# Two early output rows held back, and remainders of fills moved to GpSimd, in a four-layer attention and Fourier kernel

## The chip, the cores and the metric

The kernel runs on one core of a Trainium2 chip. Its time is the device time of one execution in microseconds (us), as the median of several runs; a profiled execution is a further run with the hardware profiler on. TensorE multiplies matrices into eight banks of PSUM, VectorE, ScalarE and GpSimd work elementwise, and SyncE (SP in the profile) issues the DMAs. Each engine takes its instructions in the order in which the program has them.

## The reference

The input x has 2048 rows of 640 values. Four layers follow each other: attention, Fourier, attention, Fourier.

```python
def _A_ref(x, wqkv, wo):
    H = 32; Dh = D // H; W = 256
    q, k, v = ...                      # x @ wqkv, 32 heads of 20
    scores = einsum("bhqd,bhkd->bhqk", q, k) * (Dh ** -0.5)
    mask = (idx[:, None] - idx[None, :] >= 0) & (idx[:, None] - idx[None, :] < W)
    p = softmax(where(mask, scores, -1e9))
    o = einsum("bhqk,bhkd->bhqd", p, v)
    return o.transpose(...).reshape(B, S, D) @ wo

def _B_ref(x, dft_seq_re, dft_seq_im, dft_hid_re, dft_hid_im):
    a = einsum("bsd,ed->bse", x, dft_hid_re)
    b = einsum("bsd,ed->bse", x, dft_hid_im)
    return einsum("ts,bse->bte", dft_seq_re, a) - einsum("ts,bse->bte", dft_seq_im, b)

x = x + _A_ref(_layernorm(x), A_wqkv, A_wo)
x = x + _B_ref(_layernorm(x), ...)
x = x + _A_ref(_layernorm(x), A_wqkv, A_wo)
x = x + _B_ref(_layernorm(x), ...)
```

## The kernel before, in words

Every product of two float32 matrices is made of three products of parts: each operand is split into a rounded part (hi) and a remainder (lo = value - hi), and hi x hi, hi x lo and lo x hi are summed in one PSUM bank. ScalarE usually makes the hi part and another engine the remainder. Many instructions on VectorE, ScalarE and GpSimd are such pairs.

**An attention layer** has four stretches. `before_heads` computes V and the first Q and K columns. `heads` is a software-pipelined loop over 8 quads of heads times 16 blocks of 128 query rows, so 128 steps after ten lead steps (`LEAD`). In a step TensorE makes four score products for the row maxima (`s_head`, line 622), whose maxima VectorE takes (line 627); four transposed score products (`t_pair`, line 650), whose exponentials ScalarE takes (line 660) and whose band GpSimd masks (`t_mask`, lines 666 and 670); and the products of the previous step's probabilities with V (`pv`, line 685).

Between these, `fill` puts pieces of other work on TensorE, once a step. First come the remaining Q and K columns: ten chunks of 128 columns, of which chunks 2 to 9 are made here (`pieces`, `lockstep`, line 253, 64-row half products in pairs), with four results of 128 x 512 each, so 32 results a layer. ScalarE copies a result out (line 540), GpSimd rounds it into the tile `c` (line 543), VectorE makes the remainder (`sub_job`, line 207), and SP stores both to `qk_d` (line 520), from where `pack` loads them into `qp` and `kp` for a later quad (line 585).

Next come the early output rows (`partials`): 16 row blocks, each the product of the first three fifths of o with `wo` (`EARLY = 3`, 36 half products), added to the layer's input (line 970). Last come the late output rows (`late`): the other two fifths (12 products), added to that (line 1064 inside the loop, 1070 after it), then mean, variance and normalization. The operands of both are loaded from `o_d` by `load_o` in sets of four row blocks, scaled by the reciprocal row sums (line 885, two halves on GpSimd, or line 873), cut into hi and lo (lines 215 and 207).

`after_heads` makes what is left of the early rows, then the late rows, and between them the first products of the Fourier layer (`unit`, `seq`, line 1360), which need normalized rows. `gather` (lines 1412 to 1431) copies the Fourier accumulators out.

**How order is set.** The order is written out by hand through a clock of half steps: `tick` advances `self.slot`, runs what `post(delay, fn)` has put off, and takes one job from each of three queues (`lanes` act, dve, pool). `job` appends to a queue, or runs the function at once when the loop is over (`self.after`). After the loop, `spend` turns estimated TensorE time into ticks.

```python
for lane in self.lanes.values():
    if lane and lane[0][0] <= self.slot:
        lane.popleft()[2]()
```

The choice of fill in the loop is `more`: projections, then all early rows, then late rows while their operands are ready. The function `fourier_hook` takes over tiles for the Fourier layer as late rows finish.

Of the kernel before, what the change touches and what calls it, by code (L numbers as in the profile page):

```python
# [8 lines left out]
F32R = mybir.dt.float32r  # L9
BF16 = mybir.dt.bfloat16  # L10
AF = mybir.ActivationFunctionType
OP = mybir.AluOpType
# [22 lines left out]
RATE = 4  # L35
FIRST = 7
LATE = 9
PACE = 0.65

STEP = 2.5  # L40
# [23 lines left out]
class Net:  # L64
# [107 lines left out]
    def tick(self):  # L172
        self.slot += 1
        for k in sorted(k for k in self.posted if k <= self.slot):
            for f in self.posted.pop(k):
                f()
        for lane in self.lanes.values():
            if lane and lane[0][0] <= self.slot:
                lane.popleft()[2]()

    def job(self, lane, key, fn):

        if self.slot is None or self.after:
            fn()
        else:
            self.lanes[lane].append((self.slot + 1, key, fn))
# [11 lines left out]
    def sub_job(self, lane, key, lo, src, hi, done=None):  # L198

        eng = {"dve": self.nc.vector, "pool": self.nc.gpsimd}[lane]  # L200
        n = 2 if lane == "pool" else 1
        w = src.shape[-1] // n
        for i in range(n):
            c = slice(i * w, (i + 1) * w)

            def sub(c=c, last=i == n - 1):
                eng.tensor_tensor(out=lo[..., c], in0=src[..., c], in1=hi[..., c].bitcast(F32), op=OP.subtract)  # L207
                if last and done:
                    done()
            self.job(lane, key, sub)  # L210
# [141 lines left out]
    def attention(self, xsrc, xdst):  # L352
        self.take_small(F32)
        for name in ("kp", "qp"):
            for i in (1, 0):
                if (name, i) != ("kp", 0):
                    self.take_qk(name, i)
        self.after, self.wide, self.lead = False, False, True
        self.late_o, self.late_t, self.part_t, self.packable = [], 0, 0, set()
        self.before_heads(xsrc)  # L360
        self.heads(xsrc, xdst, self.fourier_hook)
        self.after_heads()
# [160 lines left out]
    def pieces(self, c, sbs, role):  # L523

        self.flush(("w", c))
        w = self.turn["w", c]
        sets, of = [], {}
        for sb in sbs:
            xt = self.xnt(sb)
            if sb % 2 == 0:  # L530
                sets.append(([], []))
            p = self.bank(role)
            of[id(p)] = p, sb, self.last_bank
            sets[-1][0].append(p)
            sets[-1][1].append([((w[:, 0, k, :], w[:, 1, k, :]), (xt[:, 0, k, :], xt[:, 1, k, :])) for k in range(KC)])

        def copied(p, sb):
            st = self.work.tile([P, 2, 512], F32R, name="c", tag="c", bufs=3)
            r = self.raw()[:, :512]
            self.nc.scalar.activation(r, p, AF.Copy)  # L540

            def cast():
                self.nc.gpsimd.tensor_copy(st[:, 0, :], r)  # L543
# [3 lines left out]
            def store():  # L547
                self.store_qk(c, sb, st)
                self.packable.add((c, sb))
            self.job("pool", ("qk", c, sb), cast)  # L550
# [46 lines left out]
    def heads(self, xsrc, xdst, hook):  # L597
# [123 lines left out]
        self.rest = self.late(xsrc, xdst, hook)  # L721
        self.stored = set()
        self.slot = 0
        made = [0]
        early = 6 * EARLY * NB

        def relieve():
            while self.heavy:
# [2 lines left out]
        def more():  # L731

            r = next(self.proj, None)
            if r is not None:
                done[0] += r
                return r
            if not self.left and not self.ready_part():
                return None
            r = next(self.out, None)
            if r is not None:  # L740
                made[0] += r
                return r
            return next(self.rest, None) if self.left or self.ready_late() else None

        def fill(n):

# [21 lines left out]
        steps = 16 * NQ  # L768
        self.ring6 = dict.fromkeys((0, 1, 2, 3), -99.0)
        for step in range(-LEAD, steps + 1):  # L770
            now[0] = step
            clock = step * STEP
            if step == -1:
                self.ring6.update({4: -99.0, 5: -99.0})
# [18 lines left out]
            if done[0] < total:  # L793
                nf = max([FIRST if t < -2 else RATE + (t < 0)]
                         + [(d - done[0]) / max(1, at - s) for at, d in due])
            elif made[0] < early:
                nf = LATE
# [37 lines left out]
    def load_o(self, o, sb, k, raw=None, rr=None):  # L835

        nc = self.nc
        h0, h1, d0, d1 = CHUNKS[k]
        o["left"] = o.get("left", 0) + 1
        if not self.after and not all((q, sb) in self.stored for q in range(h0 // 4, h1 // 4)):  # L840
            def again():
                o["left"] -= 1
                self.load_o(o, sb, k, raw, rr)
            self.post(1, again)
            return
        for q in range(h0 // 4, h1 // 4):
# [36 lines left out]
        def half(i):  # L883
            cs = slice(i * 256, (i + 1) * 256)
            nc.gpsimd.tensor_tensor(out=raw[:, cs], in0=raw[:, cs], in1=rr[:, cs], op=OP.mult)
            if i:
                parts()
        for i in range(2):
            self.post(7, lambda i=i: self.job("pool", key, lambda: half(i)))

    def let_go(self):

# [104 lines left out]
    def poll_late(self, n):  # L997
# [16 lines left out]
            self.cut_to(0)  # L1014
        sb = len(self.late_o)
        if (n > 6 and sb < NSB and (NQ - 1, sb) in self.stored and (self.after or sb < 2)
                and (sb < 3 or self.late_t >= 8) and not (0 < sb < 3 and self.late_o[-1]["left"])):
            self.late_load()

    def ready_late(self):  # L1020
# [76 lines left out]
    def spend(self, us):  # L1097
        self.spent += us
        while self.spent >= PACE:
            self.spent -= PACE  # L1100
            self.tick()

    def after_heads(self):
# [227 lines left out]
    def seq(self, n):  # L1331
# [59 lines left out]
    def gather(self, sb, part, ph):  # L1391
# [20 lines left out]
                nc.scalar.activation(m1[i], banks("m1")[i], AF.Copy)  # L1412
            nc.scalar.activation(mid, banks("c1")[0], AF.Copy)
        if ph in ("a", "a2"):
            nc.scalar.activation(m5[0], banks("m5")[0], AF.Copy)
            nc.vector.tensor_copy(m5[1], banks("m5")[1])
        if ph == "b":
            out = self.raw()[:, :512]
            add(nc.vector, out, banks("c2")[0], mid)
# [3 lines left out]
                nc.scalar.activation(m7[i], banks("m7")[i], AF.Copy)  # L1423
            release("m7")
            for i in range(2):
                nc.vector.tensor_copy(m35[i], banks("m5")[i])
            release("m5")
        if ph == "g":
            for i in range(2):
# [21 lines left out]

    def fourier_hook(self, t):
        if t == 0:
            self.xa = [p.rearrange("p (l c) -> p l c", l=2) for i in (0, 1) for p in cuts(self.take_big(i), 2 * D)]
# [355 lines left out]
```

## Time and profile before

| | us |
|---|---|
| median of 3 runs | 2225.57 (2224.36 to 2226.0) |
| profiled execution | 2220.75 |
| its span | 2219.0 |
| PE busy | 2131.4 (96%) |
| VectorE busy | 1669.5 (75%) |
| ScalarE busy | 1126.6 (51%) |
| GpSimd busy | 910.6 (41%) |

The profiled execution's own time is its span and 1.75 us around it. In the rows of the profile, PE is TensorE's products and PEld its weight loads, DVE is VectorE, ACT ScalarE and POOL GpSimd. A row of the timeline has the start and the length in us, the engine, the line of the kernel, the operation, the output and the input; in brackets stands the idle time before it and what ended it. A row of a group has the count behind x, then the busy time in us and the mean of one in ns, then the idle time before it.

### The profile page before, as it was taken

To read this page: it belongs to the slowest core of one execution; us is meant where nothing else is said; L and a number is where in the kernel's file an instruction comes from. 1 tells how busy PE (TensorE), PEld (TensorE's weight loads), DVE (VectorE), ACT (ScalarE), POOL (GpSimd) and SP (SyncE) were. 2 spreads that over 40 slices of the span, in tenths; PEclk is the share of its full clock that TensorE was granted. 3 is DMA by queue.
4 is the path that set the end of the run, shared out by engine and by line. 5 is a ranking of instruction groups with operands and counts; after the bars stand their busy time and mean duration, and the time that the engine had idled before them with its cause. 6 is when DMAs were issued, how large, how long until landed. Compare 5 with 4: busy or idle time off the path is not lost.

```text
span 2219.0 us, 49084 instructions
## 1 busy us (share of the span) xinstructions
PE 2131.4 (96%) x17908; PEld 1786.0 (80%) x17908; DVE 1669.5 (75%) x4031; ACT 1126.6 (51%) x2101; POOL 910.6 (41%) x1456
## 2 busy tenths in 40 slices
PE   7999999998989999999999999998989999999999
PEld 7987777677868888889999777776777688888899
DVE  7368888785897968776651788887858978687776
ACT  3127776656554545552431377676655545455332
POOL 3016565666613223232330266566665132341334
PEclk9999999899999999999999999999999999999999
DMA  5545565775435354665646456657855354546653
GB/s 196 176 160 190 182 190 192 225 208 175 142 124 176 128 185 133 215 202 193 205 147 191 151 189 183 199 184 225 211 160 157 115 182 137 174 143 216 223 169 120
DMA packets 220177, 392.11 MB, mean 177 GB/s; under 512 B 39200, under 2 KB 85792, under 8 KB 219936
## 3 DMA queue, kind: packets, MB, share of 16 engines
q1 hardware_dynamic: 219936, 388.98, 55.6%
q8 instruction: 141, 2.31, 0.5%
q14 instruction: 100, 0.82, 0.1%
HBM read 273.94 MB, written 113.77 MB: 175 GB/s over the span
## 4 chain that ended last, share of the span: by engine, by line
PE 70%; DVE 13%; issue 6%; DMA 4%; ACT 3%; POOL 3%; SPq 0%; ACTq 0%; DVEq 0%; POOLq 0%
PE banks L1360 28%; PE banks L235 13%; PE banks L253 9%; PE banks L685 5%; PE banks L650 5%; DVE banks L627 5%; PE banks L1648 4%; PE banks L622 4%; DMA qp<-qk_d 1%; DVE c L207 1%; POOL big L228 1%; DVE mc L627 1%; DMA qk_d<-c 1%; DVE qp L228 1%; PE banks L337 1%
## 5 line engine op out<-in xcount | busy, mean ns | idle before, releaser
L627 DVE CUSTOM_DVE_ANT_0 banks<-banks,mask 128x384 f32<-128x384 f32 (+2 forms) x1024 | 526.8, 556 | 98.5 <-PE banks L622 80.5
L660 ACT ACTIVATE pt<-banks 128x768 f32<-128x768 f32 (+2 forms) x512 | 394.3, 772 | 179.0 <-PE banks L650 74.0
L666 POOL TENSOR_SCALAR_AFFINE_SELECT pt<-pt 128x256 f32<-128x256 f32 x512 | 215.8, 422 | 282.0 <-ACT pt L660 243.2
L253 PE MATMUL banks<-big,wc 64*128 64x512 f32 x1920 | 271.2, 394 | 0.4 <-DVE pt L438 0.4
L650 PE MATMUL banks<-qp,kp 61*128 61x384 f32 (+2 forms) x1024 | 211.8, 383 | 32.5 <-DVE mc L627 28.5
L685 PE MATMUL banks<-pt,vq 128*32 128x128 f32 x5760 | 213.4, 280 | 1.5 <-ACT pt L660 1.5
L622 PE MATMUL banks<-kp,qp 60*128 60x384 f32 (+2 forms) x1024 | 204.9, 352 | 6.6 <-DVE mc L627 4.1
L670 POOL TENSOR_SCALAR_AFFINE_SELECT pt<-pt 128x256 f32<-128x256 f32 x448 | 207.2, 462 | 0.0
L253 PEld LDWEIGHTS banks<-big,wc 64*128 64x128 f32 x1920 | 186.5, 185 | 22.9 <-ACT x L540 1.7
L650 PEld LDWEIGHTS banks<-qp,kp 61*128 61x128 f32 x1024 | 108.6, 186 | 100.4 <-DVE mc L627 76.5
L685 PEld LDWEIGHTS banks<-pt,vq 128*32 128x32 f32 x5760 | 143.4, 110 | 49.5 <-issue 36.4
L222 ACT ACTIVATE c<-pt 128x512 fp32r<-128x512 f32 x150 | 93.6, 626 | 160.3 <-POOL pt L1280 52.9
L222 ACT ACTIVATE qp<-pt 128x512 fp32r<-128x512 f32 (+1 forms) x195 | 119.9, 624 | 105.3 <-DVE pt L1294 54.0
L228 DVE TENSOR_TENSOR c<-pt,c 128x512 fp32r<-128x512 f32 x150 | 123.0, 822 | 52.0 <-ACT c L222 49.9
L228 DVE TENSOR_TENSOR qp<-pt,qp 128x512 fp32r<-128x512 f32 (+1 forms) x191 | 151.2, 799 | 11.7 <-ACT qp L222 9.0
L1360 PE MATMUL banks<-qp,big 128*128 128x512 f32 x630 | 152.4, 394 | 2.9 <-POOL qp L228 1.7
L1293 POOL TENSOR_TENSOR pt<-pt,pt 128x512 f32<-128x512 f32 x34 | 50.7, 1490 | 237.1 <-DMA pt<-c 145.9
L622 PEld LDWEIGHTS banks<-kp,qp 60*128 60x128 f32 x1024 | 119.9, 188 | 32.1 <-DVE mc L627 19.5
L627 DVE DVE_READ_ACCUMULATOR2_ANT mc<- 128x1 f32 x1024 | 144.3, 141 | 0.0
L1360 PEld LDWEIGHTS banks<-qp,big 128*128 128x128 f32 x630 | 119.0, 190 | 28.8 <-POOL qp L228 2.3
L1360 PE MATMUL banks<-qp,xc 128*128 128x512 f32 x480 | 117.2, 390 | 0.7 <-DVE xc L228 0.7
L543 POOL CAST c<-x 128x512 fp32r<-128x512 f32 x64 | 40.3, 633 | 181.3 <-ACT x L540 180.3
(246 smaller groups left out, 4475.0 us busy)
## 6 DMA issues: line engine op xcount, KB each, us to landing
pt<-c SPq DMA_DIRECT2D x188, 512.0 KB
qk_d<-c SPq DMA_DIRECT2D x80, 512.0 KB
kp<-qk_d SPq DMA_DIRECT2D x384, 80.0 KB
qp<-qk_d SPq DMA_DIRECT2D x384, 80.0 KB
kp<-u_d SPq DMA_DIRECT2D x32, 640.0 KB
o_d<-ou SPq DMA_DIRECT2D x64, 256.0 KB
x_d<-x SPq DMA_DIRECT2D x48, 320.0 KB
v_d<-pt SPq DMA_DIRECT2D x16, 768.0 KB
```

What stands on the lines that cost most here:

```text
L222: nc.scalar.activation(hi, src, AF.Copy, scale=-1.0 if neg else 1.0)
L228: (eng or nc.vector).tensor_tensor(out=lo, in0=src, in1=hi.bitcast(F32), op=OP.subtract)
L235: self.nc.tensor.matmul(p, x, y, start=n == 0, stop=n == last)
L253: self.nc.tensor.matmul(ps[a], x[r], y[r], start=half + i == 0, stop=half == 1 and i == n - 1, skip_group_check=True)
L622: nc.tensor.matmul(p, qp[quad % 2][b:b + 60, z, qb * P:(qb + 1) * P], kp[quad % 2][b:b + 60, z, k0 * P:(qb + 1) * P], start=True, stop=True)
L627: nc.vector.tensor_tensor_reduce(out=p, in0=p, in1=self.mask[:, 384 - n * P:], scale=1.0, scalar=NEG, op0=OP.add, op1=OP.max, accum_out=mc ...
L650: nc.tensor.matmul(self.banks[:, banks[e], :n * P], kp[quad % 2][b:b + 61, z, kb * P:(kb + 1) * P], qp[quad % 2][b:b + 61, z, kb * P:(kb + ...
L660: nc.scalar.activation(pt[quad, kb][:, 2 * z:2 * z + 2, :n * P], self.banks[:, b0:b1 + 1, :n * P], AF.Exp, scale=SCALE)
L666: nc.gpsimd.affine_select(out=t[:, :, 0:P], in_=t[:, :, 0:P], pattern=[[0, 2], [1, P]], compare_op=OP.is_ge, fill=0.0, base=0, channel_mul ...
L670: nc.gpsimd.affine_select(out=t[:, :, 256:384], in_=t[:, :, 256:384], pattern=[[0, 2], [-1, P]], compare_op=OP.is_gt, fill=0.0, base=0, ch ...
L685: nc.tensor.matmul(self.banks[32 * h:32 * h + 32, bank, :P], vq[:, 96 * (kb % 4) + 21 * h:96 * (kb % 4) + 21 * h + 32], t[:, h, (qb - kb) ...
L1360: nc.tensor.matmul(self.banks[:, bk, :], p, b[q], start=start and m == 0, stop=stop and last and m == 2, skip_group_check=True)
```

## The change

1. `copied` puts the remainder of a fill's result on GpSimd instead of VectorE, as two halves of 256 columns that are two jobs of the pool queue, and takes the tile `c` only when the rounding runs; with three tiles out it tries again a half step later. In the lead steps `tick` takes two jobs from each queue.
2. `more` takes 14 of the 16 early rows (`NB - BACK`), then two late rows, and nothing more in the loop. `after_heads` then makes early rows 14 and 15 as plain products (`in_turn`) ahead of the other late rows.
3. `load_o` scales in two halves on GpSimd while the loop has score products left, and afterwards in one operation on VectorE.
4. `job` queues after the loop as well.
5. The fourth late set is loaded when six late rows are done, not eight; the operands of the units "b7" are split one unit sooner.
6. `gather` makes its copies of the banks of `m5` (one in phases a and a2, two in phase b) on ScalarE instead of VectorE.
7. `fourier_hook` puts the split rows into the tiles `big[1]` and `big[0]` as they are, without taking new ones.

```diff
@@ tick
-            if lane and lane[0][0] <= self.slot:
-                lane.popleft()[2]()
+            for _ in range(2 if self.lead else 1):
+                if lane and lane[0][0] <= self.slot:
+                    lane.popleft()[2]()
@@ job
-        if self.slot is None or self.after:
+        if self.slot is None:
@@ sub_job
-        n = 2 if lane == "pool" else 1
+        n = 2 if lane == "pool" and len(src.shape) == 2 else 1
@@ copied (in pieces)
-            def cast():
+            def lead():
+                if self.c_live == 3:
+                    self.post(1, lambda: self.job("pool", key, lead))
+                    return
+                self.c_live += 1
+                st = self.work.tile([P, 2, 512], F32R, name="c", tag="c", bufs=3)
                 self.nc.gpsimd.tensor_copy(st[:, 0, :], r)
-                self.sub_job("dve", ("qk", c, sb), st[:, 1, :], r, st[:, 0, :],
-                             lambda: self.post(2, store))
+                self.sub_job("pool", key, st[:, 1, :], r, st[:, 0, :], lambda: self.post(2, lambda: store(st)))
@@ more (in heads)
-            if not self.left and not self.ready_part():
-                return None
-            r = next(self.out, None)
...
-            return next(self.rest, None) if self.left or self.ready_late() else None
+            if not self.left:
+                if self.part_t < NB - BACK:
+                    self.now = self.out if self.ready_part() else None
+                else:
+                    self.now = self.rest if self.late_t < BACK and self.ready_late() else None
+            return next(self.now, None) if self.now else None
@@ load_o
-        def half(i):
-            cs = slice(i * 256, (i + 1) * 256)
-            nc.gpsimd.tensor_tensor(out=raw[:, cs], in0=raw[:, cs], in1=rr[:, cs], op=OP.mult)
-            if i:
+        busy = self.step + LEAD < 16 * NQ
+        n, lane, eng = (2, "pool", nc.gpsimd) if busy else (1, "dve", nc.vector)
+
+        def scale(i):
+            cs = slice(i * 512 // n, (i + 1) * 512 // n)
+            eng.tensor_tensor(out=raw[:, cs], in0=raw[:, cs], in1=rr[:, cs], op=OP.mult)
+            if i == n - 1:
                 parts()
@@ poll_late
-                and (sb < 3 or self.late_t >= 8) and ...
+                and (sb < 3 or self.late_t >= 6) and ...
@@ after_heads
-        for _ in self.out:
+        while self.left:
+            next(self.now)
             self.spend(0.147)
+            if self.left == 0:
+                next(self.now)
+        while self.one_part():
+            pass
@@ seq
-        if self.order[n + 2:n + 3] and self.order[n + 2][2:] == ("g", 0):
+        if self.order[n + 2:n + 3] and self.order[n + 2][2:] in (("g", 0), ("b7", 0), ("b7", 1)):
@@ gather
         if ph in ("a", "a2"):
-            nc.scalar.activation(m5[0], banks("m5")[0], AF.Copy)
-            nc.vector.tensor_copy(m5[1], banks("m5")[1])
+            for i in range(2):
+                nc.scalar.activation(m5[i], banks("m5")[i], AF.Copy)
...
-                nc.vector.tensor_copy(m35[i], banks("m5")[i])
+                nc.scalar.activation(m35[i], banks("m5")[i], AF.Copy)
@@ fourier_hook
-            self.xa = [... for i in (0, 1) for p in cuts(self.take_big(i), 2 * D)]
+            self.xa = [... for i in (1, 0) for p in cuts(self.big[i], 2 * D)]
```

`one_part` is new: it takes the generator `out` to the end of one early row and spends 0.147 us of the clock for each product.

More of the change, by code (lines that the diff above doesn't have):

```diff
@@ L37 @@
 LATE = 9
+BACK = 2
 PACE = 0.65
@@ L357, in attention @@
                     self.take_qk(name, i)
-        self.after, self.wide, self.lead = False, False, True
-        self.late_o, self.late_t, self.part_t, self.packable = [], 0, 0, set()
+        self.after, self.wide, self.lead, self.step = False, False, True, 0
+        self.late_o, self.late_t, self.part_t, self.packable, self.c_live = [], 0, 0, set(), 0
         self.before_heads(xsrc)
@@ L723, in heads @@
         self.slot = 0
-        made = [0]
-        early = 6 * EARLY * NB
         def relieve():
@@ L770, in heads @@
         for step in range(-LEAD, steps + 1):
-            now[0] = step
+            now[0] = self.step = step
             clock = step * STEP
@@ L881, in parts @@
             self.cut_job("pool" if k == 0 else "dve", key, hi, lo, raw, lambda: self.post(0 if k < EARLY else 3, done))
-        def half(i):
-            cs = slice(i * 256, (i + 1) * 256)
-            nc.gpsimd.tensor_tensor(out=raw[:, cs], in0=raw[:, cs], in1=rr[:, cs], op=OP.mult)
-            if i:
+        busy = self.step + LEAD < 16 * NQ
[4 more added lines that the diff above has]
+            if i == n - 1:
                 parts()
-        for i in range(2):
-            self.post(7, lambda i=i: self.job("pool", key, lambda: half(i)))
+        for i in range(n):
+            self.post(7, lambda i=i: self.job(lane, key, lambda: scale(i)))
     def let_go(self):
@@ L1016, in poll_late @@
         if (n > 6 and sb < NSB and (NQ - 1, sb) in self.stored and (self.after or sb < 2)
-                and (sb < 3 or self.late_t >= 8) and not (0 < sb < 3 and self.late_o[-1]["left"])):
+                and (sb < 3 or self.late_t >= 6) and not (0 < sb < 3 and self.late_o[-1]["left"])):
             self.late_load()
@@ L1101, in spend, with one_part @@
             self.tick()
+    def one_part(self):
+        some = False
+        for r in self.out:
+            some = True
+            if r == 0:
+                break
+            self.spend(0.147)
+        return some
     def after_heads(self):
         self.after, self.spent = True, 0.0
-        for _ in self.out:
+        while self.left:
+            next(self.now)
             self.spend(0.147)
+            if self.left == 0:
+                next(self.now)
+        while self.one_part():
+            pass
         self.load_to(4 if self.late_t < 8 else 6)
@@ L1453, in fourier_hook @@
         if t == 0:
-            self.xa = [p.rearrange("p (l c) -> p l c", l=2) for i in (0, 1) for p in cuts(self.take_big(i), 2 * D)]
+            self.xa = [p.rearrange("p (l c) -> p l c", l=2) for i in (1, 0) for p in cuts(self.big[i], 2 * D)]
         if t == 4:
```

12 lines of the change are left out of this document (4 added, 8 removed).

## The prediction

> **What bounds the kernel now.** I read the page first, then the windows for the place of idle TensorE time, then TensorE's timeline with the waits, and last the groups for prices.
>
> ```profile
> span 2219.0 us, 49084 instructions
> PE 2131.4 (96%) x17908; PEld 1786.0 (80%) x17908; DVE 1669.5 (75%) x4031; ACT 1126.6 (51%) x2101; POOL 910.6 (41%) x1456
> PE   7999999998989999999999999998989999999999
> ```
>
> TensorE sets the pace; the last line (40 slices) shows that it is short of work mostly where a heads loop ends, once in each attention layer. The two layers run the same program, so I work out one (its heads loop lies at 157 to 538 us) and double it.
>
> In the heads loop I take the start of each block of 24 L685 products (the probabilities times V, one block a step) as the clock of the steps:
>
> ```profile
> 247.15 0.86 PE L685 MATMUL banks<-pt,vq 128*32 128x128 f32 x24
> 255.26 0.64 PE L685 MATMUL banks<-pt,vq 128*32 128x128 f32 x16
> 302.55 0.86 PE L685 MATMUL banks<-pt,vq 128*32 128x128 f32 x24
> 303.50 0.41 POOL L666 TENSOR_SCALAR_AFFINE_SELECT pt<-pt 128x256 f32<-128x256 f32 x1
> 303.58 0.87 DVE L207 TENSOR_TENSOR c<-x,c 128x512 fp32r<-128x512 f32 x1
> 303.86 0.86 POOL L670 TENSOR_SCALAR_AFFINE_SELECT pt<-pt 128x256 f32<-128x256 f32 x1
> 305.36 0.82 DVE L207 TENSOR_TENSOR c<-x,c 128x512 fp32r<-128x512 f32 x1
> 305.45 0.86 PE L685 MATMUL banks<-pt,vq 128*32 128x128 f32 x24
> 311.83 0.86 PE L685 MATMUL banks<-pt,vq 128*32 128x128 f32 x24
> ```
>
> Three steps without a remainder take 8.11 us (247.15 to 255.26), three with two of them on VectorE 9.28 (302.55 to 311.83), each with 24 fill products and one transpose. The waits of TensorE in the loop (us in total, times, longest) name the same engine:
>
> ```profile
> PE banks L650 <- DVE mc L627: 8.6, 21, 0.5
> PE banks L622 <- DVE mc L627: 0.5, 1, 0.5
> ```
>
> VectorE's maxima (L627) hold the bank that TensorE wants next, and the remainder stands in front of them.
>
> **Part 1: remainders of fills go from VectorE to GpSimd, in halves.**
>
> ```profile
> L207 DVE TENSOR_TENSOR c<-x,c 128x512 fp32r<-128x512 f32 x64 | 53.0, 828 | 0.4
> L207 POOL TENSOR_TENSOR big<-x,big 128x256 fp32r<-128x256 f32 x16 | 11.8, 737 | 0.0
> L543 POOL CAST c<-x 128x512 fp32r<-128x512 f32 x64 | 40.3, 633 | 181.3 <-ACT x L540 180.3 <-DMA qk_d<-c 0.5 <-ACT wc L215 0.4
> L627 DVE CUSTOM_DVE_ANT_0 banks<-banks,mask 128x384 f32<-128x384 f32 (+2 forms) x1024 | 526.8, 556 | 98.5 <-PE banks L622 80.5 <-PE banks L650 0.3
> 406.64 0.41 POOL L666 TENSOR_SCALAR_AFFINE_SELECT pt<-pt 128x256 f32<-128x256 f32 x1 [0.19 <-ACT pt L660]
> 407.38 0.73 POOL L885 TENSOR_TENSOR x<-x,rr 128x256 f32<-128x256 f32 x1
> 408.06 0.41 POOL L666 TENSOR_SCALAR_AFFINE_SELECT pt<-pt 128x256 f32<-128x256 f32 x1
> ```
>
> Per layer 32 x 0.828 = 26.5 us leave VectorE and 64 halves x 0.737 = 47.2 us come to GpSimd. Eight of the 32 fall in the ten lead steps, where GpSimd makes no masks yet: 8 x (0.633 + 2 x 0.737) = 16.9 us, beside TensorE's solid fills. I count nothing there; two jobs a half step keep its queue short. The other 24 come in 12 pairs. By the steps a pair costs 9.28 - 8.11 = 1.17 us, 14 us a layer; by the waits it is 8.6 + 0.5 = 9.1. The difference is VectorE's delay inside blocks whose ends are modelled, and ScalarE's copies, which stay. I take 9; the ceiling is 14.
>
> What could take it back is GpSimd, where a half stands ahead of the masks that L685 needs. The nearest rows are those of the scalings L885, also 256 wide and between masks: from mask to mask 1.42 us (406.64 to 408.06), with a half step of 8.11 / 6 = 1.35. So the queue falls 0.07 behind in each of six half steps, 0.4 in all. The mask that ends at 303.91 is first read at 305.45: slack 1.54 us. So the lag stays hidden; if it did not, it would be the rival below. The store of a remainder moves one or two half steps back on SP, past six loads that don't need it, and the transfers of the next quad keep eight steps of lead: nothing.
>
> Does the half on GpSimd slow L627? A mask beside a remainder on VectorE takes 0.86 us instead of 0.41 (303.86), and that goes. [...]
>
> **Part 2: the heads' end.**
>
> ```profile
> 526.47 0.86 PE L685 MATMUL banks<-pt,vq 128*32 128x128 f32 x24
> 532.19 0.86 PE L685 MATMUL banks<-pt,vq 128*32 128x128 f32 x24
> 537.34 0.86 PE L685 MATMUL banks<-pt,vq 128*32 128x128 f32 x24
> 544.60 2.79 POOL L885 TENSOR_TENSOR cr<-cr,rr 128x256 f32<-128x256 f32 x4
> 546.72 2.06 DVE L207 TENSOR_TENSOR kp<-cr,kp 128x512 fp32r<-128x512 f32 x2 [2.11 <-ACT kp L215]
> 549.23 1.15 PE L235 MATMUL banks<-qp,kp 128*128 128x320 f32 x6 [3.59 <-DVE x L1070]
> 571.69 1.92 PE L235 MATMUL banks<-qp,kp 128*128 128x320 f32 x12
> PE banks L235 <- DVE x L1070: 4.9, 4, 3.6
> 545.00:550.00 5.00, 1.41 (x10) 1.15 (x9) 3.10 (x5) 3.14 (x6) 3.49 (x5) 1.00 1.00 357
> 550.00:560.00 10.00, 9.37 (x35) 8.04 (x34) 8.28 (x22) 7.13 (x14) 5.86 (x7) 0.66 0.46 156
> 560.00:580.00 20.00, 19.82 (x110) 17.60 (x109) 19.58 (x46) 7.69 (x14) 9.05 (x10) 1.00 0.63 202
> ```
>
> In the rows of windows stand busy PE, PEld, DVE, ACT and POOL, then the clock. After the last step the scalings of the second late set sit on GpSimd (544.60, four of them in a row), ScalarE's cut waits for them, VectorE's for that, the sum L1070 stands behind it, and TensorE waits 3.59 us for its bank, 4.9 in all. The granted clock then falls to 0.66 for ten microseconds: 3.4 more. Gross 8.3 us.
>
> The change takes 14 early rows as paired half products, then two late rows, and leaves early rows 14 and 15 as 36 plain products for after the last step. Two steps lose their fill: 5.72 us (526.47 to 532.19) become two steps that TensorE's score products and the exponentials set; with fill they take 2.86, with TensorE's work alone about half. I take 2.0 each: 1.7 less. The next two carry 12 products instead of 9: 6 x 0.16 (1.92 / 12) = 1.0 more. Afterwards 36 x 0.16 = 5.8 come and the two late rows' 24 x 0.16 = 3.8 go. Sum 1.3 more, so TensorE gains 8.3 - 1.3 = 7.0. These 5.8 us are the cover for the scalings, which are now one VectorE operation each, from a queue that lets the row's sum pass. Where they wait, the sum of early row 14 and then the late rows' sums stand behind them on VectorE. But VectorE is next: idle for 1.9 and 1.7 us from 545 to 560, and 98% busy from 560 to 580, so it gives back about 3.6 and no more unless its work shrinks. I take 5, between 3.6 and 7.0; the best is 8.3. The rest of the end (the fourth set loaded two rows earlier, the Fourier operands put into the old tiles without a new allocation) has no price of its own: TensorE is full there.
>
> **Part 3: the start of the Fourier layer.**
>
> ```profile
> 605.00:645.00 40.00, 36.56 (x147) 26.00 (x146) 35.76 (x80) 22.00 (x53) 4.80 (x4) 1.00 0.41 127
> 645.00:660.00 15.00, 11.54 (x48) 8.33 (x47) 14.69 (x22) 8.17 (x16) 3.13 (x2) 1.00 0.39 120
> L1426 DVE COPY kp<-banks 128x512 f32<-128x512 f32 x16 | 10.4, 684 | 0.2
> L1423 ACT ACTIVATE kp<-banks 128x512 f32<-128x512 f32 x16 | 8.8, 589 | 0.3
> ```
>
> TensorE idles 3.4 + 3.5 = 6.9 us here while VectorE is 89% and then 98% busy. In this block three copies go to ScalarE: 3 x 0.684 = 2.05 us off VectorE. Splitting the operand of two "b7" units one unit sooner may save another 0.5. I take 2.5; the ceiling is 4, and at worst two copies behind two others on ScalarE (2 x 0.589) release their banks 1 us late. In the other blocks TensorE is full (slices at 9), so the copies count nothing there.
>
> **Sum.** 9 + 5 + 2.5 = 16.5 us a layer, 33 for two. The profiled execution took 2220.75 us (its span of 2219.0 and 1.75 around it): 2187.8. The median of the runs is 2225.57, 4.8 above it, so I predict 2192.6 on the median's scale.
>
> **The rivals.** (A) The gain of part 1 goes to another engine: ScalarE's copies and GpSimd's masks hold the pairs of steps at 9.28.
>
> ```profile
> 406.99 0.86 PE L685 MATMUL banks<-pt,vq 128*32 128x128 f32 x24
> 413.06 0.86 PE L685 MATMUL banks<-pt,vq 128*32 128x128 f32 x24
> ```
>
> For it: these two steps, with scalings on GpSimd, two cuts on ScalarE and no remainder on VectorE, take 3.04 us each, against 2.70 in the three without any. Against it: most pairs have no such cuts. Then 7.5 a layer are left, 15 in all: 2210.6. Chance 0.17.
>
> (B) Slower: GpSimd becomes the bound. If masks keep 0.86 beside the halves, a half step there is 0.41 + 0.86 + 0.74 = 2.0 us against 1.35, a lag of 0.66 x 6 = 4.0 a pair, 2.4 above the slack of 1.54. A pair then costs 2.4 instead of 1.17: 12 x 1.2 = 15 more a layer, less 7.5 from the rest, twice: 2240. It decides when a half step on GpSimd passes 1.35 + 1.54 / 6 = 1.61 us. Against it stands 1.42. Chance 0.11. [...]
>
> (C) The two steps without fill cost the clock, as they did in the same layer's earlier steps without fill:
>
> ```profile
> 420.00:437.00 17.00, 15.29 (x145) 10.32 (x147) 11.24 (x41) 7.42 (x15) 7.19 (x17) 0.52 0.79 245
> ```
>
> Such a stretch costs 17 x 0.48 = 8.2 us. Part 2 is then 3 us worse than nothing, and the sum 8.3 a layer: 2209. Against it: two steps, not five, and full work behind them. Chance 0.10. [...]
>
> **How the numbers follow.** The forecast has 0.62; all of it is faster. A measurement of this kernel can tell about 0.2% from no change, 4.5 us. Of A 0.15 and of C 0.08 are faster and 0.02 each the same; of B 0.09 slower, 0.02 the same. So faster 0.85, same 0.06, slower 0.09. The best of all three parts (14 + 8.3 + 4, twice 26.3) gives 2173; A and C lie at 2209 to 2211, and with part 3 at nothing at 2216. I give 2174 to 2218, which leaves B out.
>
> **What would show it.** Waits of L650 and L622 on L627 should fall from 9.1 us to under 2, and triples of steps with a pair to about 8.4. Masks on GpSimd should stay near 0.41. The wait of 3.59 us and the clock of 0.66 after the last step should be gone, and VectorE near full until the late rows end. TensorE's idle time from 605 to 660 should fall to about 4.5. I am wrong if L685 waits for GpSimd's masks in the loop, or the clock falls in the thin steps.

## The result and the profile after

The changed kernel takes 2200.86 us (median of 4 runs, 2197.0 to 2201.15), the kernel before beside it 2224.97: ratio 0.9889, 95% interval 0.9871 to 0.9906. On another chip it was 2203.68 against 2222.33, ratio 0.9908 (0.9893 to 0.9923). It is faster by 19 to 24 us, where 33 were forecast. Of all runs here one lies more than 0.5% from the median of its kernel, 4749 us with part 3 alone, and that ratio leaves it out. Lines of the page after:

```profile
span 2199.4 us, 48840 instructions
PE 2127.3 (97%) x17872; PEld 1785.7 (81%) x17872; DVE 1620.9 (74%) x3949; ACT 1139.1 (52%) x2125; POOL 969.0 (44%) x1568
PE   7999999998999999999999999999999999999999
```

VectorE has 49 us less to do and GpSimd 58 more. Of the four slices of 8 at the heads' ends one is left. The triple of steps that the prediction showed with remainders began its steps at 302.55, 305.45 and 308.70 and ended at 311.83. The one of these four rows that the prediction does not show:

```profile
308.70 0.86 PE L685 MATMUL banks<-pt,vq 128*32 128x128 f32 x24
```

The same triple in the timeline after (the first row shows 12 of the 24 products of its block):

```profile
301.88 0.54 PE L692 MATMUL banks<-pt,vq 128*32 128x128 f32 x12
304.80 0.86 PE L692 MATMUL banks<-pt,vq 128*32 128x128 f32 x24
307.48 0.86 PE L692 MATMUL banks<-pt,vq 128*32 128x128 f32 x24
310.60 0.86 PE L692 MATMUL banks<-pt,vq 128*32 128x128 f32 x24
```

2.92, 2.68 and 3.12 us, 8.72 in all, where before had 2.90, 3.25 and 3.13. One step of the three became shorter. The waits of TensorE in the loop (us in total, times, longest), again over about the first 91 steps, and the groups of GpSimd that the rivals were about:

```profile
PE banks L657 <- DVE mc L634: 3.0, 9, 0.6
PE banks L629 <- DVE mc L634: 0.4, 1, 0.4
...
L673 POOL TENSOR_SCALAR_AFFINE_SELECT pt<-pt 128x256 f32<-128x256 f32 x512 | 214.7, 420 | 217.5 <-ACT pt L667 197.8
L677 POOL TENSOR_SCALAR_AFFINE_SELECT pt<-pt 128x256 f32<-128x256 f32 x448 | 194.0, 433 | 0.0
L209 POOL TENSOR_TENSOR c<-x,c 128x256 fp32r<-128x256 f32 x128 | 95.0, 749 | 0.0
```

The wait of 9.1 us is 3.4 now. A half costs 0.749 us, and the masks stay at 0.42 to 0.43. L666 and L670 before, L673 and L677 after, are the same two masks. The waits of TensorE's products for the early rows held back and the late rows (L235 before, L237 after) behind the last step, first before (537 to 660 us), then after (533 to 650):

```profile
PE banks L235 <- DVE x L1070: 6.6, 5, 3.6
```

```profile
PE banks L237 <- DVE x L1075: 1.8, 1, 1.8
PE banks L237 <- DVE big L975: 1.7, 1, 1.7
PE banks L237 <- ACT big L224: 1.0, 1, 1.0
```

The thin steps, which go without fill (timeline, then a window with busy PE, PEld, DVE, ACT, POOL and the clock):

```profile
520.68 0.86 PE L692 MATMUL banks<-pt,vq 128*32 128x128 f32 x24
523.46 0.86 PE L692 MATMUL banks<-pt,vq 128*32 128x128 f32 x24 [1.07 <-ACT pt L667]
525.38 1.10 PE L692 MATMUL banks<-pt,vq 128*32 128x128 f32 x24 [0.28 <-ACT pt L667]
530.13 0.86 PE L692 MATMUL banks<-pt,vq 128*32 128x128 f32 x24
532.88 0.86 PE L692 MATMUL banks<-pt,vq 128*32 128x128 f32 x24
...
525.00:530.00 5.00, 4.71 (x42) 3.93 (x40) 0.52 (x2) 1.48 (x4) 1.23 (x4) 0.66 0.69 199
```

The stall on the row sums (L1070 before, L1075 and L975 after) fell from 6.6 us to 3.5, and 1.0 us on ScalarE's cut is new. But behind the two thin steps (2.78 and 1.92) the clock drops, and the step that should take about 3.3 takes 4.75. I number steps from 1, the one that begins with the loop's first block of L692; the thin ones are 124 and 125, the slow one 126.

### The profile page after: what moved, and what is told of

It reads as the page before. It is cut to its first block, busy times and chain, and to the rows that moved or that the text cites. A ratio compares the mean times of both kernels' runs of the same rounds, so it can differ in the third digit from the quotient of the medians.

```text
span 2199.4 us, 48840 instructions
## 1 busy us (share of the span) xinstructions
PE 2127.3 (97%) x17872; PEld 1785.7 (81%) x17872; DVE 1620.9 (74%) x3949; ACT 1139.1 (52%) x2125; POOL 969.0 (44%) x1568
## 4 chain that ended last, share of the span: by engine, by line
PE 79%; DVE 7%; ACT 4%; DMA 4%; POOL 3%; issue 3%; SPq 0%; ACTq 0%; DVEq 0%; POOLq 0%
PE banks L1380 29%; PE banks L237 15%; PE banks L255 13%; PE banks L692 6%; PE banks L657 5%; PE banks L1668 5%; PE banks L629 4%; DVE banks L634 1%; DMA qp<-qk_d 1%; DVE qp L230 1%; ACT pt L667 1%; DMA qk_d<-c 1%; PE banks L339 1%; POOL rs L1084 1%; ACT big L1036 1%
## 5 line engine op out<-in xcount | busy, mean ns | idle before, releaser
L634 DVE CUSTOM_DVE_ANT_0 banks<-banks,mask 128x384 f32<-128x384 f32 (+2 forms) x1024 | 527.4, 557 | 120.2 <-PE banks L629 97.3
L673 POOL TENSOR_SCALAR_AFFINE_SELECT pt<-pt 128x256 f32<-128x256 f32 x512 | 214.7, 420 | 217.5 <-ACT pt L667 197.8
L657 PE MATMUL banks<-qp,kp 61*128 61x384 f32 (+2 forms) x1024 | 210.8, 382 | 24.8 <-DVE mc L634 17.6
L692 PE MATMUL banks<-pt,vq 128*32 128x128 f32 x5760 | 212.0, 278 | 3.5 <-ACT pt L667 3.5
L677 POOL TENSOR_SCALAR_AFFINE_SELECT pt<-pt 128x256 f32<-128x256 f32 x448 | 194.0, 433 | 0.0
L692 PEld LDWEIGHTS banks<-pt,vq 128*32 128x32 f32 x5760 | 142.5, 110 | 51.4 <-issue 35.6
L657 PEld LDWEIGHTS banks<-qp,kp 61*128 61x128 f32 x1024 | 108.6, 185 | 90.0 <-DVE mc L634 63.9
L1380 PE MATMUL banks<-qp,big 128*128 128x512 f32 x648 | 154.5, 392 | 0.0
L634 DVE DVE_READ_ACCUMULATOR2_ANT mc<- 128x1 f32 x1024 | 145.0, 142 | 0.0
L1380 PEld LDWEIGHTS banks<-qp,big 128*128 128x128 f32 x648 | 121.5, 189 | 25.2 <-POOL qp L230 0.9
L230 DVE TENSOR_TENSOR c<-pt,c 128x512 fp32r<-128x512 f32 x142 | 113.9, 804 | 26.9 <-ACT c L224 24.3
L1380 PE MATMUL banks<-qp,xc 128*128 128x512 f32 x480 | 119.0, 394 | 6.5 <-DVE xc L230 3.7
L1380 PEld LDWEIGHTS banks<-qp,xc 128*128 128x128 f32 x480 | 90.2, 189 | 28.5 <-DVE xc L230 6.3
```

Of the source, the lines that this page charges most:

```text
L230: (eng or nc.vector).tensor_tensor(out=lo, in0=src, in1=hi.bitcast(F32), op=OP.subtract)
L634: nc.vector.tensor_tensor_reduce(out=p, in0=p, in1=self.mask[:, 384 - n * P:], scale=1.0, scalar=NEG, op0=OP.add, op1=OP.max, accum_out=mc ...
L657: nc.tensor.matmul(self.banks[:, banks[e], :n * P], kp[quad % 2][b:b + 61, z, kb * P:(kb + 1) * P], qp[quad % 2][b:b + 61, z, kb * P:(kb + ...
L673: nc.gpsimd.affine_select(out=t[:, :, 0:P], in_=t[:, :, 0:P], pattern=[[0, 2], [1, P]], compare_op=OP.is_ge, fill=0.0, base=0, channel_mul ...
L677: nc.gpsimd.affine_select(out=t[:, :, 256:384], in_=t[:, :, 256:384], pattern=[[0, 2], [-1, P]], compare_op=OP.is_gt, fill=0.0, base=0, ch ...
L692: nc.tensor.matmul(self.banks[32 * h:32 * h + 32, bank, :P], vq[:, 96 * (kb % 4) + 21 * h:96 * (kb % 4) + 21 * h + 32], t[:, h, (qb - kb) ...
```

## The experiments

Each ratio is to the kernel before, run beside it. In the experiments' profiles line numbers may be a few off those of the changed kernel.

**Part 1 alone**

```diff
 (before)
-                self.sub_job("dve", ("qk", c, sb), st[:, 1, :], r, st[:, 0, :],
-                             lambda: self.post(2, store))
+                self.sub_job("pool", key, st[:, 1, :], r, st[:, 0, :], lambda: self.post(2, lambda: store(st)))
```

> The kernel before with part 1 alone: remainders of fills on GpSimd in halves, two jobs a half step in the lead. The prediction has 9 us a layer, 18 in all: 2207. The theory after the result: part 1 is worth only the waits that it took away in the changed kernel's loop (8.6 to 3.0 us) and a little inside blocks, 6 us a layer, 12 in all: 2213. Rival: part 1 is worth nearly the whole gain and parts 2 and 3 cancel: under 2204.

2210.78, ratio 0.9935 (0.9922 to 0.9947): 14.2 us (11.8 to 17.4 by the interval), 7.1 a layer, between the two numbers. By the timelines, steps 1 to 90 take 252.2 and 252.1 us in the two layers of the kernel before and 246.3 in both here, 5.8 less. Steps 91 to 97 take 26.2 and 25.0 before, 24.5 and 23.8 here.

**No remainders at all**

```diff
 (changed)
-                self.sub_job("pool", key, st[:, 1, :], r, st[:, 0, :], lambda: self.post(2, lambda: store(st)))
+                self.job("pool", key, lambda: None)
+                self.job("pool", key, lambda: self.post(2, lambda: store(st)))
```

> The changed kernel without the remainders of fills: neither engine makes them, and the rounded part is stored in their place. If the halves on GpSimd hold back what a pair still costs, triples of steps with a pair fall from 8.5 to 8.7 us to 8.1, like those without. If ScalarE's copies and the weight chunks' remainders on VectorE do, the triples stay within 0.1 of 8.5 to 8.7.

The triple of the prediction in this kernel, and its wait over the same stretch of the loop:

```profile
302.57 0.86 PE L695 MATMUL banks<-pt,vq 128*32 128x128 f32 x24
305.46 0.86 PE L695 MATMUL banks<-pt,vq 128*32 128x128 f32 x24
308.11 0.86 PE L695 MATMUL banks<-pt,vq 128*32 128x128 f32 x24
311.30 0.86 PE L695 MATMUL banks<-pt,vq 128*32 128x128 f32 x24
...
PE banks L660 <- DVE mc L637: 2.7, 8, 0.6
```

2.89, 2.65 and 3.19: 8.73, although no engine makes a remainder. The middle step, 2.68 with halves on GpSimd, is 2.65 without them, so GpSimd holds back 0.03 us. What stays above 8.11 is not the remainder's. For the same stretch, steps 1 to 90, the wait of the t_pair products alone (L650, L657, L660) is 8.2 us before, 3.0 after and 2.7 here, so 2.7 us of it are not the remainder's either. These steps take 247.6 and 247.4 us here, no less than with the halves on GpSimd (246.4 and 246.3). (Two stores instead of one go out per result here, and the third step is the longer for it or for another reason; that stays open, and so does its single time of 2206.82.)

**Part 2 alone**

```diff
 (before)
+BACK = 2
+                if self.part_t < NB - BACK: ...
+        n, lane, eng = (2, "pool", nc.gpsimd) if busy else (1, "dve", nc.vector)
-        if self.slot is None or self.after:
+        if self.slot is None:
```

> The kernel before with part 2 alone: two early rows held back, late scalings on VectorE, queues kept on after the loop, the fourth late set two rows sooner, the Fourier operands put into the old tiles. The prediction has 5 us a layer, 10 in all: 2215. The theory after the result: 3.4 us a layer, since the two steps without fill cost a clock of 0.66 in the step behind them, 1.3 to 2.6 us, and the stretch after the loop gains 5 to 6: 2218. Rival: part 2 rests on part 1 (VectorE free of remainders), alone it gives nothing: 2225.

2215.93, ratio 0.9959 (0.9947 to 0.9971): 9.1 us (6.5 to 11.8), near the 10 of the prediction. It doesn't need part 1. The thin steps cost nothing here: steps 124 to 127 take 2.77, 1.93, 3.26 and 2.74 in the first layer, 10.70 against 10.87 before, and 10.71 in the other. So the dip that the theory priced was not there in either layer, though its sum of 7 us lies just inside the interval.

To compare what follows, I take one stretch by the timelines: from the start of step 124 to the start of the 230th product of the Fourier layer (L1360 before, L1380 after), which is 99 us behind the last step before and comes after all products of the late rows. It takes 109.7 us in both layers of the kernel before, and 106.1 and 105.2 here: 4.0 a layer less.

**Part 3 alone**

```diff
 (before)
-            nc.vector.tensor_copy(m5[1], banks("m5")[1])
+                nc.scalar.activation(m5[i], banks("m5")[i], AF.Copy)
-                nc.vector.tensor_copy(m35[i], banks("m5")[i])
+                nc.scalar.activation(m35[i], banks("m5")[i], AF.Copy)
```

> The kernel before with part 3 alone: three copies of each accumulator block on ScalarE, operands of two units split one unit sooner. The prediction has 2.5 us a layer, 5 in all: 2220. The theory after the result, from the stretch between the first and the long L1380 block, which is 36.55 us before and 36.59 after: nothing, 2225. Rival: ScalarE releases the banks later and it costs 1 us a layer: 2227.

2220.29, ratio 0.9981 (0.9972 to 0.9991): 4.2 us by the ratio (2.0 to 6.2), 4.7 by the medians, again near the prediction's number and not that of the theory after the result, which had looked at the wrong place. Windows of this kernel and, in the second fence, of the kernel before, 60 to 90 us after the last step:

```profile
597.26:627.26 30.00, 27.51 (x121) 21.05 (x120) 24.66 (x57) 15.83 (x37) 10.49 (x12) 1.00 0.33 102
```

```profile
597.34:627.34 30.00, 26.56 (x114) 19.46 (x114) 23.80 (x54) 15.48 (x36) 10.49 (x12) 1.00 0.31 93
```

TensorE is busy 0.95 us longer in the same 30 us, and 0.99 in the second layer; the stall in the 35 us behind that stays (3.5 us in both). The stretch from step 124 to the 230th Fourier product takes 108.2 and 107.9 us, 1.5 and 1.8 less than before, so the traces place 3.3 of the gain there.

**The pieces of part 2, each undone**

```diff
-BACK = 2
+BACK = 0
```

> The changed kernel without the hold-back (16 early rows in the loop, no late row there); late scalings stay on VectorE, the queues stay on after the loop. The theory that the 36 plain products after the last step cover the scalings: the wait for them returns in part (3.6 us a layer less what VectorE saves, against 1.3 for the thin steps), 2 a layer slower: 2205. Rival: the queues and the faster scalings carry part 2 and the two thin steps only cost (step 126 takes 4.75 and 5.74 us in the changed kernel at a clock of 0.5 to 0.66, 3.26 without the dip): 2 a layer faster: 2197.

```diff
-        busy = self.step + LEAD < 16 * NQ
-        n, lane, eng = (2, "pool", nc.gpsimd) if busy else (1, "dve", nc.vector)
+        n, lane, eng = 2, "pool", nc.gpsimd
```

> The changed kernel with the late scalings in two halves on GpSimd also at the loop's end. The prediction's step: VectorE is the next bound after the loop; four scalings of 0.89 us a layer leave it, but two halves of 0.79 come later in the chain before ScalarE's cut: the wait on the row sums grows by 1 to 2 us a layer: 2204. Rival: the 36 plain products cover the scalings wherever they are, and VectorE's load is what counts: 1 to 2 us a layer faster: 2198.

```diff
-        if self.slot is None:
+        if self.slot is None or self.after:
```

> The changed kernel with jobs run at once after the loop, as in the kernel before. The prediction's step: the queue lets the sum of an early row pass the scalings and remainders. If that counts, the sum L975 stands behind a scaling, a cut and a remainder and TensorE waits 1 to 3 us more a layer: 2203 to 2207. Rival: the order of VectorE's work there doesn't matter, since the same work has to be done: 2201.

| | us | ratio | over the changed kernel |
|---|---|---|---|
| no hold-back | 2206.31 | 0.9917 (0.9903 to 0.9931) | 0.0018 |
| scaling on GpSimd | 2211.41 | 0.9943 (0.9930 to 0.9957) | 0.0044 |
| jobs at once | 2210.27 | 0.9929 (0.9916 to 0.9942) | 0.0030 |

The last column stands against 0.9899, the mean of the changed kernel's two ratios, whose half-width is about 0.0012 (of two of 0.0018 and 0.0015, as a root of squares, halved). With that of each experiment the differences are uncertain by 0.0018, so leaving out the scaling or the queue is shown to cost time, and more than was expected; for the hold-back the uncertainty is as large as the difference. The waits on the row sums after the last step of the first layer, in this order:

```profile
PE banks L237 <- DVE x L1075: 5.8, 6, 2.6
```

```profile
PE banks L237 <- DVE x L1074: 5.7, 3, 3.2
```

```profile
PE banks L237 <- DVE x L1075: 6.4, 4, 2.9
```

Each piece left out brings this wait from 3.5 us back to about 6, near the 6.6 of before (the changed kernel has 1.0 us on ScalarE's cut beside it, these three none). The wait is not the whole cost. The stretch from step 124 to the 230th Fourier product takes 106.2 to 106.6 us in the four layers of the changed kernel's two profiles. It takes 107.6 and 106.6 without the hold-back, 111.5 and 110.1 with the scaling on GpSimd, and 111.7 and 107.6 with jobs at once, against 109.7 before. Some of this is the clock: it is granted at 0.50 for 6.8 us of the stretch in each layer of the changed kernel, and for 13.7 and 10.2 us, and 13.7 and 6.8, in the last two. By their ratios parts 1 and 3 alone would make 0.9916 together (uncertain by 0.0016), and none of the three versions is faster than that, so with any one piece left out no gain of part 2 is seen. The pieces don't add up, they need each other: the products cover the scalings only if these are short and if a row's sum may pass them. The rivals (VectorE's load, or only the cost of the thin steps) fall.

**A new version: one row held back, two late rows in the loop**

```diff
-BACK = 2
+BACK = 1
-                    self.now = self.rest if self.late_t < BACK and self.ready_late() else None
+                    self.now = self.rest if self.late_t < 2 and self.ready_late() else None
```

> A new version: the changed kernel with 15 early rows and two late rows in the loop, so that one early row (18 plain products) is held back and the first of the two thin steps, and the second, get the 15th row's halves. Theory: the two steps of 2.78 and 1.93 us take 5.7 instead of 4.7, step 126 comes without the clock's dip (3.26 for 4.75 and 5.74) and 18 x 0.16 = 2.9 us less are left after the loop: 3 to 4 us a layer faster, 2193. Rival: the held-back row is cover that VectorE needs after the loop, so what leaves TensorE comes back as a wait: 2199 to 2202.

2204.6, ratio 0.9911 (0.9897 to 0.9924): no gain. The loop's end does what the theory says, with 3.28 us for step 126 in both layers. But the wait comes back:

```profile
PE banks L237 <- DVE x L1075: 5.5, 2, 3.1
```

All waits of the L237 products there, that on ScalarE's cut included, are 5.5 and 5.2 us in the two layers, against 3.5 to 4.5 in four of the changed kernel, and the stretch to the 230th Fourier product takes 106.1 and 105.6 us although it has 2.9 us less work. 18 products are not cover enough; the rival holds.

**New versions: part 1's idea for the early operand sets**

```diff
-            self.cut_job("pool" if k == 0 else "dve", key, hi, lo, raw, ...
+            self.cut_job("pool" if k == 0 or k < EARLY and sb in (1, 2) else "dve", key, hi, lo, raw, ...
```

> A new version: the changed kernel with all remainders of the early operand sets 1 and 2 on GpSimd in halves (so far one of three), as part 1 did with the fills. In steps 98 to 123 TensorE waits 4.6 us a layer on VectorE's maxima, up to 1.4 at a time, behind a row's sum of 0.82 and such a remainder of 0.73. Theory: four remainders a layer leave, and with them some 2 us of this wait: 4 in all, 2197. Rival: GpSimd is 81% busy at 470 to 480 us and makes masks late, or the operand sets come later: no gain or slower, 2200 to 2206.

> As the version with sets 1 and 2, but all four early sets: set 3 is cut where GpSimd is 98% busy (500 to 510 us) and VectorE 62%. Theory: set 3 gains nothing on VectorE and delays masks: 1 to 2 us a layer slower than with sets 1 and 2, 2199 to 2201. Rival: only VectorE counts: 1 us a layer faster than it, 2195.

2222.51, ratio 0.9989 (0.9977 to 1.0), and 2219.64, ratio 0.9983 (0.9970 to 0.9996). In both the operand sets seem to come too late for their rows, since the halves lengthen the pool queue (the next version, which shortens it, bears this out): the early rows last to steps 124 to 127 (2.91, 2.79, 2.85 and 2.30 us with sets 1 and 2, as in the kernel before), and no late rows are made in the loop. Both also put out wrong values, and why was not found, so no more is read from these two than this. Neither theory had the queue in it; the first one's rival named late operand sets, at 2200 to 2206.

```diff
+            for _ in range(2 if self.lead or len(lane) > 3 else 1):   # tick, beside the edit for sets 1 and 2
```

> A new version: the changed kernel with all remainders of the early operand sets 1 and 2 on GpSimd, and two jobs a half step from a queue that holds more than three, so that the operand sets are complete in the same step as in the changed kernel and TensorE's order is the same. Theory (VectorE is what steps 98 to 123 wait for): four remainders of 0.73 us a layer leave it; the wait of L657 on the maxima falls from 4.6 us a layer to under 3: 2197. Rival: two halves in a row on GpSimd, 1.5 us, make the masks late, and what VectorE gives is lost there: 2201 or more.

> The changed kernel once more, on the same chip as the version with early remainders on GpSimd: 2201, as the standard of comparison. Where step 126 holds a dip of the clock it takes 4.7 to 5.8 us, without it 3.26.

The new version takes 2201.3, ratio 0.9905 (0.9890 to 0.9920), the changed kernel beside it 2203.68, 0.9908: no difference that the runs can tell (0.0003, uncertain by 0.0021). Waits of steps 98 to 123 (447 to 521 us), first of the changed kernel in its first profile, then of the new version:

```profile
PE banks L657 <- DVE mc L634: 4.6, 9, 1.4
```

```profile
PE banks L657 <- DVE mc L634: 1.9, 6, 0.4
PE banks L629 <- ACT pt L667: 1.4, 2, 1.0
PE banks L692 <- POOL pt L673: 0.8, 1, 0.8
```

VectorE's wait falls by 2.7 us as expected, and 2.2 us of waits on ScalarE's exponentials and GpSimd's masks take its place. Steps 104 and 112, which had stood behind the remainders, fall from 4.49 to 3.39 and from 4.05 to 3.40, but 102 and 110, in which remainders now run on GpSimd two halves in a row (1.44 us at 450.27 and 1.43 at 477.29), rise from 2.93 to 3.59 and from 3.11 to 4.14. Steps 98 to 123 take 84.8 and 84.5 us, where the changed kernel has 84.2 to 85.8 in four layers. This is what rival A of the prediction feared (the gain goes to another engine), at another place; for the fills it didn't happen, here it did.

**The clock's dip.** The changed kernel's second run shows the same thin steps with and without it. Windows of 3.41 us, the length of the shortest dips, the first two in the first layer, the others in the second:

```profile
523.69:527.10 3.41, 2.06 (x32) 1.19 (x32) 2.03 (x4) 2.87 (x7) 2.76 (x6) 1.00 0.39 118
527.10:530.51 3.41, 3.31 (x31) 2.75 (x32) 0.00 (x0) 1.19 (x4) 1.22 (x3) 0.50 0.84 268
1612.57:1615.98 3.41, 2.79 (x46) 2.03 (x44) 2.19 (x4) 3.04 (x6) 2.00 (x5) 1.00 0.00 0
1615.98:1619.39 3.41, 2.38 (x54) 1.59 (x54) 1.11 (x3) 2.66 (x5) 2.57 (x7) 1.00 0.69 193
```

In the first layer the idle time of the thin steps falls into one window (2.06 busy), and the next runs at 0.50: step 126 takes 4.71. In the second it is shared by two windows (2.79 and 2.38), the clock holds, and it takes 3.26. Six profiled runs have just these thin steps, in twelve layers: in seven step 126 takes 3.26, in five 4.71 to 5.74. On the grid of windows on which the dips of a run lie (last section), the emptiest window there had 2.04 to 2.13 us of busy TensorE in the five, and 2.14 to 2.44 in the seven; the two groups lie too close together to name a limit.

## Why the prediction was right, and where its sizes were off

The direction and the mechanisms were right. By the parts run alone, the terms were 18, 10 and 5 us for two layers and measured 14.2, 9.1 and 4.7. One sign of being wrong did come, "or the clock falls in the thin steps": it fell there in three of the changed kernel's four layers, at 1.5 to 2.8 us a layer.

**Part 1, the step that was mis-sized: "by the waits it is 8.6 + 0.5 = 9.1 ... I take 9".** It is 7.1 a layer (5.9 to 8.7): 5.8 in steps 1 to 90, the same in every layer, and perhaps 1.3 in steps 91 to 97, which take 25.6 us in the mean of six layers with remainders on VectorE and 24.3 in the mean of fourteen with them on GpSimd. A half clock comes and goes there and single layers take 22.2 to 26.5 us, so the 1.3 is not shown to be the remainders'. The step gave all of VectorE's wait to the remainders. Without any remainders 2.7 us of it are left. The ceiling of 14 came from "9.28 - 8.11 = 1.17", which compares unlike steps: the pairs always fall on the same steps of a quad's 16, and these take 8.7 us also without remainders. The gain is in the middle step alone, 3.25 - 2.68 = 0.57 here and 0.45 to 0.56 in the other ten pairs of steps 1 to 90, and these eleven make the 5.8. Triples come to 8.5 to 8.7 (the first and the last of the eleven aside, at 9.0 and 9.6), not 8.4. That GpSimd would bear the halves was right: 749 ns against the 737 that the prediction took, and masks at 0.42 to 0.43. The 9 also counts no slowing of VectorE's maxima by the halves, which no run had shown when it was written. The profile after shows none: their 128x384 form takes 582 ns in the mean (L634), and 581 before (L627). So B did not occur, and A not in the loop's fills.

**Part 2** was forecast at 5 a layer and gives 4.55 alone. The cover is shown by the row held back alone: with one instead of two, the wait on the row sums goes from 3.5 to 5.5 us and no time is gained. What the hold-back is worth beside the other pieces is less sure (0.0018, uncertain by as much). The two steps without fill take 2.78 and 1.93 us, where 2.0 each was taken. The prediction said that early row 14's sum would be what stands behind, and 1.7 of the 3.5 us are on L975, the sums of early rows. The wait of 3.59 did not go but became 1.8 and 1.7, so the best of 8.3 was never near. The clock is 1.00 from 540 to 570, where before had 0.66 from 550 to 560, but in the first layer 3.4 us at 0.50 follow the wait of 1.8, at 570.2. "VectorE near full until the late rows end" holds to 570 us (4.84 of 5 us from 545 to 550, 9.72 of 10 from 560 to 570) and not for the last 25 us of them (7.81 of 10 from 570 to 580).

**Part 3** was forecast at 2.5 a layer and gives 2.35 alone by the medians, 1.0 to 3.1 by the interval of the ratio; the traces of part 3 alone place 1.5 and 1.8 a layer. The idle time of TensorE in the 65 us that begin 60 us after the last step fell from 6.9 to 4.8 in the first layer, with 4.5 forecast for nearly the same work, but only from 6.4 to 5.6 in the second. The gain lies in the first 30 us, and the later stall, 3.5 us in the first layer, is untouched.

**The sum.** By the ratios the parts alone make 0.65 + 0.41 + 0.19 = 1.25%, the whole 1.11 and 0.92%, 1.01 in the mean: 0.24% or 5 us less, uncertain by 0.23% (the half-widths as a root of squares). So that parts are lost together is barely shown by the ratios. The timelines show where: from step 124 to the 230th Fourier product, part 2 alone saves 4.0 us a layer and part 3 alone 1.7, and the changed kernel 3.3 in the mean of four layers. That is 2.4 a layer less, 4.8 for two. In this stretch the clock is at 0.50 for 6.8 us in each of the four layers, and for 3.4 and 0 in the two of part 2 alone, which is one profiled run. So the lost time goes with half clock; that the clock is all of it is not shown, since no run sets where the dips fall. Rival C is the part of this in the thin steps. It has a chance in each layer rather than in the whole: steps 124 to 127 take 10.7 us without the dip and 12.2 to 13.5 with it, 0.93 a layer in the mean of the twelve, 1.9 for two. Part 2 alone had none there in its profiled run. The rival's price was far too high: the stretch of 17 us at 0.52 that the prediction took it from is five windows of 3.41 us in a row at 0.50 (420.6 to 437.7 us), behind windows with 2.45 to 3.12 us of busy TensorE; these steps have one or two at 0.50.

The profiled run after began its heads loop 2.5 us later than that before (165.93 against 163.39), so spans understate the gain a little; the medians don't rest on it.

## What to carry to other kernels

Compare a step with an operation only to the same step of another period without it, or leave the operation out once: neighbouring steps have other work, and a wait that names an engine holds all that this engine does, not only what you are about to move. Work held back as cover, short operations on the engine that is waited for, and a queue that lets the urgent one pass, may each be worth nothing without the others, so undo them one at a time before dropping one. The same move of remainders to the idler engine paid where only VectorE was late and paid nothing that could be told where ScalarE and GpSimd were next, 2.7 us of waiting for 2.2.

## What the runs showed of the hardware

The dips of the granted clock lie on a grid. In the first profile after they begin, the last 2 us of the span aside, at 433.70, 525.86, 570.24, 1522.55, 1614.71 and 1734.18 us, all whole multiples of 3.4133 us apart (27, 40, 319, 346 and 381 from the first, to 0.1 us), and last 3.4 or 6.8 us at 0.50. In the profile before, the span's end again aside, they begin at 420.59, 550.30, 1536.75, 1649.39 and 1755.20 us (38, 327, 360 and 391 from the first) and last 3.4, 6.8 or 17.1 us; 420.59 lies 13.11 us or 3.84 such lengths from 433.70, so the grid stands elsewhere there. In the thin steps a window of the grid still 60 to 62% busy by the profile (2.04 and 2.13 us, at 522.45 and 1611.30) stood ahead of a dip. Busy time is not the measure everywhere: in the same profile windows with 1.72 us busy at 539.51 and 1.65 at 1655.67 kept the clock, and in the profile before one with 2.45 in the earlier thin steps lost it (417.18). So the same steps pay or not as the grid falls on them: 1.5 to 2.8 us at step 126 and its neighbours, in five of the twelve layers.

Away from the dips the loop repeats closely: steps 1 to 90 take 246.2 to 246.8 us in the fourteen layers of seven runs (the changed kernel twice, part 1 alone, the three pieces undone, one row held back), and 252.1 to 252.5 in all six layers with remainders on VectorE.
